# Linear attention and a gated feed-forward in one kernel: v of the first batch loaded ahead of q, and other piece widths in feed-forward blocks 0 to 3

## Chip, cores and metric

The kernel runs on one core of one Trainium2 chip. The metric is the device time of one execution in microseconds (us). The engines of a core work side by side, each through its own instructions in order: PE multiplies matrices, DVE and ACT do element-wise work, POOL does small work and issues DMAs (loads and stores), SP issues DMAs. PEld is the loading of a matmul's stationary operand.

## The reference

Two parts follow each other. The first is a linear attention over 8 batches of 8 heads, 576 tokens and 64 values per head:

```python
r = np.maximum(x, 0.0)                                   # phi, for q and k
return np.concatenate([r * c, r * s], axis=-1)           # c, s: cos and sin of the position
kv = np.einsum('bhsf,bhsd->bhfd', k_p, v)
z = np.sum(k_p, axis=2)
num = np.einsum('bhsf,bhfd->bhsd', q_p, kv)
den = np.einsum('bhsf,bhf->bhs', q_p, z)[..., None] + 1e-06
return (num / den).astype(np.float32)
```

The second is a gated feed-forward over all 8 x 576 = 4608 tokens, 512 wide inside and 1536 in the middle:

```python
rms = np.sqrt(np.mean(x * x, axis=-1, keepdims=True) + 1e-06)
xn = x / rms * rms_g
g = xn @ w_gate
silu = g * (1.0 / (1.0 + np.exp(-g)))
val = xn @ w_val
return (silu * val @ w_out).astype(np.float32)
```

## The kernel before

**Token tiles and blocks.** A batch is cut into four token tiles of 128 tokens, (b, 0) to (b, 3), and a fifth of 64 tokens; the fifths of two batches make one tile. The four full tiles of a batch are one block of 512 tokens for the feed-forward, so blocks 0 to 7 are batches 0 to 7, and block 8 holds the fifths.

**Attention of a batch.** k, q and v come in by two DMAs each (line 117), one for the odd and one for the even partitions. The k features (`k_feat`, lines 246 and 248) and casts of v (`v_cast`, 258 and 260) go to bf16; `kv_mm` (293) multiplies them over the five tiles, `kv_evict` (307, 309, 312) copies the product from PSUM (the memory that PE writes) to SBUF. `q_feat` makes the q features of one tile and one of two halves (cos or sin) on ACT or DVE; `q_turn_pe` (329) transposes them with PE and `q_evict` (338, 340) copies the result; later tiles use a DMA transpose instead (318). `num_mm` (353) makes numerator and denominator of a tile.

**From there to the feed-forward.** `divide` (379, 382, 391: three instructions on DVE), `sumsq` (402 on ACT, then a power on POOL, 407, whose result is called rs), `norm` (412 on DVE, giving xn), then a transpose of xn: `x_turn_pe` with PE (430) and its copy `x_evict` (437 on DVE, 439 on ACT), or `x_turn` as a DMA transpose issued by SP (420). The result, xnT, is what the feed-forward multiplies.

**Feed-forward.** A block has twelve steps, numbered through: step g is step g mod 12 of block g // 12. A step makes one PSUM bank of 512 columns for the gate (gps) and one for the value (vps). In blocks 0 to 4 a step is split by the table `PARTS` (464): an entry (n, first token, tokens) says that the step takes the tokens given and as many rows of 128 features from n on as fill the bank, so four for 128 tokens, two for 256. A matmul is then 128 or 256 columns wide. In blocks 5 to 8 a step is one row of features over all 512 tokens (449). After the matmuls ACT takes silu of gps (696), DVE multiplies by vps (706) into hT. From block 2 on, each step also does four matmuls of the block before it with wo (`out_mm`, 496), whose results ACT copies (502) and SP stores (486). Between blocks 0 and 1 stands `lead` (719), in which the output of block 0 is worked out while batch 1's attention is made ready.

**Order.** Every instruction stays where the program puts it on its engine. For the steps there is a plan: `at(g, kind, f, ...)` puts f into step g at a place named by its kind. The places in a step are, in order: sp, act0, dve0, the gate matmuls, mid, the first half of the value matmuls, half, the second half, silu, act1, act2, dve1, the multiply into hT, pe. Whatever f issues goes to its own engines at that point of their order, so a step's dve0 comes after the multiply of the step before, and its act1 after its own silu. `tile_at(g, ...)` puts num at the end of step g, divide and sumsq into g + 1, norm and the DMA transpose into g + 2.

**Memory that sets waits.** The gate and value banks come from a ring of three banks, which the PE transposes of block 0 use too (`gv_tile`); a bank is free for the next user when its reader is done. One further bank, acc, holds the warm-up matmuls and later the output sums. Each weight comes in by DMAs that POOL issues (`load_gv`, `load_wo`), after a small copy (`pool_after`, 240) that makes POOL wait for a given feature.

Of the kernel before, what the change touches and what calls it, by code (L numbers as in the profile page):

```python
# [17 lines left out]
def kernel(  # L18
# [105 lines left out]
    def load_v(b, cuts=(0, NC5)):  # L124
        load(vraw[b], v, b, False, cuts)

    def load_k(b):
        load(kraw[b], k, b)

    def load_q(b, cuts=(0, NC5)):  # L130
        load(qraw[b], q, b, b % 2 == 1, cuts)
# [3 lines left out]
    clear_fifth(vbuf[0], nc.vector)  # L135
    gb = consts.tile([P, DM], FP32, name="gb")
    load_k(0)
    load_q(0, (0, 2))
    load_v(0)
    K(nc.sync.dma_start(  # L140
        out=gb[:, :], in_=moe_rms_g.rearrange("(o d) -> o d", o=1).to_broadcast([P, DM])
    ))
# [77 lines left out]
    wo = consts.tile([P, NNT, DM], BF16, name="wo")  # L220
    probe = consts.tile([1, 1], BF16, name="probe")
    NG = 3
    GC = DFF // NG
    n4 = NNT // NG

    def load_gv(c):
        for (w, src) in ((wg, moe_w_gate), (wv, moe_w_val)):
            K(nc.gpsimd.dma_start(
                out=w[:, :, c * GC : (c + 1) * GC],
                in_=src[:, c * GC : (c + 1) * GC].rearrange("(t p) n -> p t n", p=P),  # L230
            ))

    def load_wo(c):
        K(nc.gpsimd.dma_start(
            out=wo[:, c * n4 : (c + 1) * n4, :],
            in_=moe_w_out[c * n4 * P : (c + 1) * n4 * P, :].rearrange("(t p) m -> p t m", p=P),
        ))

    def pool_after(src):
        K(nc.gpsimd.tensor_copy(out=probe[:, :], in_=src))  # L240
# [60 lines left out]
    def kv_evict(b):  # L301
        dst = kvm[b % NK][:, :, :].rearrange("p (z s) w -> p z s w", z=2)
        if b == 0:
            for z, t in enumerate(kvp.pop(b)):
                src = t[:, 0 : Z * E].rearrange("p (s w) -> p s w", w=E)[:, :, 0 : D + 1]
                if z == 0:
                    K(nc.scalar.copy(out=dst[:, z, :, 0 : D + 1], in_=src))
                else:
                    K(nc.vector.tensor_copy(out=dst[:, z, :, 0 : D + 1], in_=src))
                gv_read(t)  # L310
        else:
            K(nc.scalar.copy(
                out=dst[:, :, :, 0 : D + 1], in_=att_heads(kvp.pop(b))[:, :, :, 0 : D + 1]
            ))
# [7 lines left out]

    qtp = {}

    def q_turn_pe(b, t):
        ps = gv_tile([P, H, P], BF16, "qtp")
        qp = qps.pop((b, t))
        for h in range(H):
            K(nc.tensor.transpose(  # L329
                ps[:, h, :], qp[:, h, :, :].rearrange("p c d -> p (c d)"), ident_b[:, :]  # L330
            ))
        qtp[b, t] = ps
# [90 lines left out]

    xps = {}

    def x_turn_pe(key):
        ps = gv_tile([P, NDT, P], BF16, "xps")
        xn = xns.pop(key)
        for dt in range(NDT):
            K(nc.tensor.transpose(ps[:, dt, :], xn[:, dt * P : (dt + 1) * P], ident_b[:, :]))  # L430
        xps[key] = ps
# [21 lines left out]
        return ps  # L453

    HB = TB // 2

    def gv_mm_part(w, name, blk, n0, c0, cn, half=None):

        ps = gv_tile([P, TB], FP32, name)
        for i in range(TB // cn):  # L460
            if half is not None and 2 * i == TB // cn:
                half()
            for dt in range(NDT):
                K(nc.tensor.matmul(  # L464
                    ps[:, i * cn : (i + 1) * cn],
                    lhsT=w[:, dt, (n0 + i) * P : (n0 + i + 1) * P],
                    rhs=xnT[blk][:, dt, c0 : c0 + cn],
                    start=(dt == 0), stop=(dt == NDT - 1),
                ))
        return ps  # L470
# [40 lines left out]
    def at(g, w, f, *a):  # L511
        plan[g, w].append(lambda: f(*a))
# [32 lines left out]
        at(g + 1, "act0", kv_evict, b)  # L545


    at(0, "half", x_turn_pe, (0, 1))
    at(0, "act0", sumsq, (0, 2))
    at(0, "dve0", q_feat, 0, 3, 1)  # L550
    at(0, "act1", x_evict, (0, 1), 0, 1)
    at(0, "pe", norm, (0, 2))
    at(0, "pe", q_turn_pe, 0, 3)
    at(1, "act0", q_evict, 0, 3)
    at(1, "mid", x_turn_pe, (0, 2))
    at(1, "dve1", x_evict, (0, 2), 0, 2, True)
    at(1, "mid", num_mm, (0, 3))
    at(1, "dve1", divide, (0, 3))
    at(2, "act0", sumsq, (0, 3))
    at(3, "dve0", norm, (0, 3))  # L560
    at(3, "pe", x_turn_pe, (0, 3))
    at(4, "dve0", x_evict, (0, 3), 0, 3, True)
    for c in range(2):
        at(2 + c, "act2", q_feat, 0, J, c, True)
# [42 lines left out]
    pe_tile_at(19, (2, 0), 2, 0, 22, "act0")  # L607
    for t, g in enumerate((14, 16, 20, 21, 23)):
        q2_at(g, 2, t)
    pe_tile_at(22, (2, 1), 2, 1, 24)  # L610
    tile_at(24, (2, 2), 2, 2)
    tile_at(26, (2, 3), 2, 3)

# [44 lines left out]
    def run(g, w):  # L658
        for f in plan[g, w]:
            f()  # L660


    T = [(c * P, P) for c in range(J)] + [(hf * HB, HB) for hf in range(2)]
    PARTS = {0: tuple((n,) + T[c] for n, c in (
        (0, 0), (0, 1), (0, 2), (4, 4), (6, 4), (0, 3), (4, 5), (6, 5), (8, 4), (10, 4), (8, 5),
        (10, 5),
    ))}
    for blk in (1, 2, 3, 4):
        head = (
            [(n,) + T[c] for c in range(2) for n in (0, 4, 8)] if blk < 3  # L670
            else [(n,) + T[4] for n in range(0, NNT, 2)]
        )
        PARTS[blk] = tuple(head + [(n,) + T[5] for n in range(0, NNT, 2)])

    def step(blk, nn):
        g = blk * NNT + nn
        run(g, "sp")
        run(g, "act0")
        run(g, "dve0")
        while late_turns:  # L680
            x_turn(*late_turns.pop(0))
        if nn == 0:
            hT[blk] = htp.tile([P, NNT, TB], BF16, name="hT", tag="hT")
        if blk in PARTS:
            n0, c0, cn = PARTS[blk][nn]
            ni = TB // cn
            gp = gv_mm_part(wg, "gps", blk, n0, c0, cn)
            run(g, "mid")
            vp = gv_mm_part(wv, "vps", blk, n0, c0, cn, lambda: run(g, "half"))
            dst = hT[blk][:, n0 : n0 + ni, c0 : c0 + cn]  # L690
        else:
            gp = gv_mm(wg, "gps", blk, nn)
            vp = gv_mm(wv, "vps", blk, nn)
            dst = hT[blk][:, nn, :]
        sil = ring(silp, 3, [P, TB], BF16, "sil")
        K(nc.scalar.activation(out=sil[:, :], in_=gp[:, :], func=AF.Silu))  # L696
        gv_read(gp)
        run(g, "act1")
        ends = blk > 1 and nn % 3 == 2
        if not ends:  # L700
            run(g, "act2")
# [70 lines left out]
    def warm_up(n):  # L772
        for _ in range(n):
            K(nc.tensor.matmul(
                wps[:, 0 : 2 * P], lhsT=warm[:, 0:P], rhs=warm[:, :], start=True, stop=True
            ))

    warm_up(44)
    for j in range(NC5):
        for c in range(2):  # L780
            if (j, c) in ((2, 1), (NC5 - 1, 1)):
                q_feat(0, 0, int(j > 2), act=(j > 2))
            k_feat(0, j, c, act=(j > 2))
    for c in range(2):
        q_feat(0, 1, c, act=(c == 1))
    pool_after(qps[0, 0][0:1, 0, 0, 0:1])
    for c in range(NG):
        load_gv(c)
    for c in range(2):
        load_wo(c)  # L790
    q_turn_pe(0, 0)
    q_evict(0, 0, dve=True)
    q_turn_pe(0, 1)
    q_evict(0, 1)
    warm_up(6)
    for j in range(NC5):
        v_cast(0, j, act=(j % 2 == 1))
    for j in (0, 1, 2, 4, 3):
        kv_mm(0, j, j == 0, j == 3)
    kv_evict(0)  # L800
    num_mm((0, 0))
    num_mm((0, 1))
    for c in range(2):
        q_feat(0, 2, c, act=True)
    divide((0, 0))
    warm_up(5)
    q_turn_pe(0, 2)
    warm_up(5)
    sumsq((0, 0))
    divide((0, 1))  # L810
    sumsq((0, 1))
    q_evict(0, 2, dve=True)
    norm((0, 0))
    num_mm((0, 2))
    q_feat(0, 3, 0, act=True)
    x_turn_pe((0, 0))
    divide_rec((0, 2))
    x_evict((0, 0), 0, 0, dve=True)
    divide((0, 2))
    norm((0, 1))  # L820


# [53 lines left out]
```

## Time and profile before

| | |
|---|---|
| time, median of 3 runs | 331.35 us (331.07 to 331.37) |
| the profiled execution's own time | 331.03 us |
| its span, first to last instruction | 328.9 us |
| PE busy in the span | 97% |
| first weight matmul (line 464) | 19.82 us |
| lead begins | 42.67 us |
| granted TensorE clock, mean | 0.999 |

A line of the timeline reads: start, duration, engine, source line, operation, what it writes and reads, shapes, and how many instructions were merged (x8). A bracket at the end tells how long the engine had been idle before, and what released it. In the chain of waits a line is start, duration, and what the chain went through. In a table by stretches the columns are the stretch, its length, busy time and number of instructions of PE, PEld, DVE, ACT and POOL, the granted clock, the share of DMA time and the GB/s. In the list of DMA issues the last figure is the median time in us from issue to landing.

### The profile page before, as it was taken

To read this page: it belongs to the slowest core of one execution; us is meant where nothing else is said; L and a number is where in the kernel's file an instruction comes from. 1 tells how busy PE (TensorE), PEld (TensorE's weight loads), DVE (VectorE), ACT (ScalarE), POOL (GpSimd) and SP (SyncE) were. 2 spreads that over 40 slices of the span, in tenths; PEclk is the share of its full clock that TensorE was granted. 3 is DMA by queue.
4 is the path that set the end of the run, shared out by engine and by line. 5 is a ranking of instruction groups with operands and counts; after the bars stand their busy time and mean duration, and the time that the engine had idled before them with its cause. 6 is when DMAs were issued, how large, how long until landed. Compare 5 with 4: busy or idle time off the path is not lost.

```text
span 328.9 us, 7190 instructions
## 1 busy us (share of the span) xinstructions
PE 318.6 (97%) x2840; PEld 210.5 (64%) x2840; DVE 189.7 (58%) x394; ACT 168.2 (51%) x319; POOL 40.3 (12%) x80
## 2 busy tenths in 40 slices
PE   6789999999999999999999999999999999999995
PEld 4679855999888777778777644454444444444443
DVE  4785386868875676678867685746542422223200
ACT  2865377776576466666645663644332323322221
POOL 3743351100100100001110001100100000000000
PEclk9999999999999999999999999999999999999999
DMA  7999999389469999997799895255124010000012
GB/s 215 305 206 207 287 335 385 121 200 229 148 127 261 319 256 324 189 302 177 205 185 288 174 228 142 65 91 118 49 65 111 33 49 32 35 32 32 34 64 96
DMA packets 83313, 55.26 MB, mean 168 GB/s; under 512 B 51760, under 2 KB 77120, under 8 KB 83280
## 3 DMA queue, kind: packets, MB, share of 16 engines
q1 hardware_dynamic: 76576, 42.88, 52.7%
q0 software_dynamic: 6544, 11.80, 14.8%
q8 instruction: 22, 0.36, 0.4%
q14 instruction: 11, 0.09, 0.1%
q10 hardware_dynamic: 160, 0.13, 0.1%
HBM read 38.01 MB, written 9.44 MB: 144 GB/s over the span
## 4 chain that ended last, share of the span: by engine, by line
PE 89%; DVE 4%; ACT 2%; issue 2%; DMA 2%; SPq 0%; POOL 0%; ACTq 0%; DVEq 0%
PE acc L496 26%; PE gps L464 15%; PE vps L464 15%; PE vps L449 13%; PE gps L449 13%; PE att L353 3%; PE att L293 3%; DMA kbuf<-in_k_dram 2%; DVE xn L412 1%; PE acc L838 1%; PE qtp L329 1%; PE xps L430 1%; ACT kp L246 1%; DVE x L391 1%; DVE kp L248 0%
## 5 line engine op out<-in xcount | busy, mean ns | idle before, releaser
L706 DVE TENSOR_TENSOR hT<-vps,sil 128x512 bf16<-128x512 f32 x108 | 74.5, 690 | 96.3 <-PE vps L449 62.0
L696 ACT ACTIVATE sil<-gps 128x512 bf16<-128x512 f32 x108 | 64.4, 596 | 98.5 <-PE gps L449 60.1
L496 PE MATMUL acc<-wo,hT 128*128 128x512 bf16 x420 | 105.7, 380 | 0.2 <-ACT osb L502 0.2
L496 PEld LDWEIGHTS <-hT 128*128 128x128 bf16 x420 | 40.5, 98 | 40.3 <-issue 0.3
L464 PE MATMUL gps<-xnT,wg 128*128 128x256 bf16 (+1 forms) x608 | 62.5, 250 | 0.5 <-DVE xnT L437 0.5
L464 PE MATMUL vps<-xnT,wv 128*128 128x256 bf16 (+1 forms) x608 | 62.7, 250 | 0.0
L464 PEld LDWEIGHTS <-wg 128*128 128x128 bf16 x608 | 48.0, 98 | 7.7 <-issue 0.6
L464 PEld LDWEIGHTS <-wv 128*128 128x128 bf16 x608 | 49.4, 98 | 4.0
L407 POOL TENSOR_TENSOR rs<-ss,mhalf 128x1 f32<-128x1 f32 x36 | 20.2, 562 | 199.9 <-ACT sq L402 199.9
L449 PE MATMUL vps<-xnT,wv 128*128 128x512 bf16 x144 | 37.0, 379 | 0.0
L449 PE MATMUL gps<-xnT,wg 128*128 128x512 bf16 x144 | 36.9, 379 | 0.0
L502 ACT COPY osb<-acc 128x512 f32<-128x512 f32 x35 | 20.4, 584 | 31.8 <-PE acc L496 30.5
L449 PEld LDWEIGHTS <-wv 128*128 128x128 bf16 x192 | 18.8, 98 | 22.7
L412 DVE SCALAR_TENSOR_TENSOR xn<-x,rs,gb 128x512 bf16<-128x512 f32 x36 | 27.0, 749 | 9.0 <-POOL rs L407 8.8
L449 PEld LDWEIGHTS <-wg 128*128 128x128 bf16 x192 | 18.0, 98 | 20.1
L402 ACT ACTIVATE sq<-x 128x513 f32<-128x513 f32 x36 | 22.6, 629 | 8.6 <-DVE x L391 8.4
L391 DVE TENSOR_TENSOR x<-att,rec 128x512 f32<-128x512 f32 x36 | 24.9, 691 | 1.2
L248 DVE TENSOR_SCALAR kp<-kbuf,trig 128x512 bf16<-128x512 f32 x50 | 22.6, 483 | 3.6 <-DMA kbuf<-in_k_dram 3.2
L248 DVE TENSOR_SCALAR qp<-qbuf,trig 128x512 bf16<-128x512 f32 x50 | 22.9, 481 | 0.0
L246 ACT ACTIVATE kp<-kbuf,trig 128x512 bf16<-128x512 f32 x30 | 20.8, 715 | 3.0 <-DMA kbuf<-in_k_dram 3.0
L246 ACT ACTIVATE qp<-qbuf,trig 128x512 bf16<-128x512 f32 x30 | 21.1, 712 | 0.2 <-DMA qbuf<-in_q_dram 0.2
L353 PEld LDWEIGHTS <-rqT 128*128 128x128 bf16 x320 | 14.4, 98 | 8.0 <-DVE rqT L338 0.9
(64 smaller groups left out, 182.6 us busy)
## 6 DMA issues: line engine op xcount, KB each, us to landing
out_dram<-osb SPq DMA_DIRECT2D x70, 128.0 KB, 2.1
kbuf<-in_k_dram SPq DMA_DIRECT2D x6, 640.0 KB, 5.7
vbuf<-in_v_dram SPq DMA_DIRECT2D x5, 640.0 KB, 7.7
kbuf<-in_k_dram SPq DMA_DIRECT2D x6, 512.0 KB, 4.7
qbuf<-in_q_dram SPq DMA_DIRECT2D x6, 512.0 KB, 5.0
vbuf<-in_v_dram SPq DMA_DIRECT2D x5, 512.0 KB, 6.6
qbuf<-in_q_dram SPq DMA_DIRECT2D x4, 640.0 KB, 6.5
wg<-in_moe_w_gate_dram POOLq DMA_DIRECT2D x3, 512.0 KB, 11.4
```

What stands on the lines that cost most here:

```text
L246: K(nc.scalar.activation(out=dst, in_=src, func=AF.Relu, scale=scale))
L248: K(nc.vector.tensor_scalar(out=dst, in0=src, scalar1=scale, scalar2=0.0, op0=ALU.mult, op1=ALU.max,))
L353: K(nc.tensor.matmul(nums[key][:, h // Z, (h % Z) * E : (h % Z) * E + D + 1], lhsT=rqT[a, t][:, h, :], rhs=kvm[a % NK][:, h, 0 : D + 1], s ...
L391: K(nc.vector.tensor_tensor(out=x[:, 0:DM].rearrange("p (z s d) -> p z s d", z=2, d=D), in0=a[:, :, :, 0:D], in1=r.unsqueeze(3).to_broadca ...
L402: K(nc.scalar.activation(out=sq[:, :], in_=xs[key][:, :], func=AF.Square, scale=1.0 / math.sqrt(DM), accum_out=ss[:, :],))
L412: K(nc.vector.scalar_tensor_tensor(out=xn[:, :], in0=xs.pop(key)[:, 0:DM], scalar=rss.pop(key)[:, :], in1=gb[:, :], op0=ALU.mult, op1=ALU. ...
L449: K(nc.tensor.matmul(ps[:, :], lhsT=w[:, dt, nn * P : (nn + 1) * P], rhs=xnT[blk][:, dt, :], start=(dt == 0), stop=(dt == NDT - 1),))
L464: K(nc.tensor.matmul(ps[:, i * cn : (i + 1) * cn], lhsT=w[:, dt, (n0 + i) * P : (n0 + i + 1) * P], rhs=xnT[blk][:, dt, c0 : c0 + cn], star ...
L496: K(nc.tensor.matmul(acc[blk][:, :], lhsT=hT[blk][:, nn, jt * P : (jt + 1) * P], rhs=wo[:, nn, :], start=(nn == 0), stop=(nn == NNT - 1),))
L502: K(nc.scalar.copy(out=osb[:, :], in_=acc[blk][:, :]))
L696: K(nc.scalar.activation(out=sil[:, :], in_=gp[:, :], func=AF.Silu))
L706: K(nc.vector.tensor_tensor(out=dst, in0=a, in1=c, op=ALU.mult))
```

## The change

On SP the load of v of batch 0 stands ahead of the first columns of q. The first features and casts are in another order: all of k, then v's casts and kv, then the q features of tiles (0,0) and (0,1), then `kv_evict`, whose halves also swap engines. The first weights come in pieces of 256 columns (two rows of features), four for each of the two matrices, and the remaining third and the first two of wo are issued later. The probe that releases them reads a k feature instead of a q feature. Warm-up matmuls are set anew (52, 3, 12 instead of 44, 6, 5, 5).

In block 0 the first step is a pair: rows 0 and 1 over tokens 0 to 127, and then, in the same step and banks, over tokens 128 to 255 (`gv_mm_pair`). Into its first half go num of tile (0,2) and the transpose of tile (0,1). The three PE transposes of xn and the q transpose planned in block 0's steps use the bank acc instead of the ring. Divide of (0,3) moves from step 1's dve1 to step 2's dve0.

The table of pieces: block 1 has a pair, then five steps of 256 tokens from the first half, then six of the second; block 2 has four 128-token steps instead of six; block 3 has three steps of tokens 0 to 255, three of tokens 256 to 511, and then six of all 512. Block 4 is as it was.

```diff
     load_k(0)
+    load_v(0)
     load_q(0, (0, 2))
-    load_v(0)
...
-    def load_gv(c):
+    def load_gv(lo, hi):
+
+        cs = slice(lo * P, hi * P)
...
+    def gv_mm_pair(blk, n0, between, half):
+
+        gp, vp = (gv_tile([P, TB], FP32, name) for name in ("gps", "vps"))
+        for c in range(2):
+            for w, ps in ((wg, gp), (wv, vp)):
+                if c == 0 and w is wv:
+                    between()
+                for i in range(2):
+                    if c == 0 and w is wv and i == 1:
+                        half()
+                    for dt in range(NDT):
+                        K(nc.tensor.matmul(
+                            ps[:, i * HB + c * P : i * HB + (c + 1) * P],
+                            lhsT=w[:, dt, (n0 + i) * P : (n0 + i + 1) * P],
+                            rhs=xnT[blk][:, dt, c * P : (c + 1) * P],
+                            start=(dt == 0), stop=(dt == NDT - 1),
+                        ))
+        return gp, vp
...
-    at(0, "half", x_turn_pe, (0, 1))
-    at(0, "act0", sumsq, (0, 2))
-    at(0, "dve0", q_feat, 0, 3, 1)
-    at(0, "act1", x_evict, (0, 1), 0, 1)
-    at(0, "pe", norm, (0, 2))
-    at(0, "pe", q_turn_pe, 0, 3)
-    at(1, "act0", q_evict, 0, 3)
-    at(1, "mid", x_turn_pe, (0, 2))
-    at(1, "dve1", x_evict, (0, 2), 0, 2, True)
-    at(1, "mid", num_mm, (0, 3))
-    at(1, "dve1", divide, (0, 3))
-    at(2, "act0", sumsq, (0, 3))
+    at(0, "mid", num_mm, (0, 2))
+    at(0, "half", x_turn_pe, (0, 1), True)
+    at(0, "half", x_evict, (0, 1), 0, 1)
+    at(0, "half", divide, (0, 2))
+    at(0, "half", sumsq, (0, 2))
+    at(0, "half", q_feat, 0, 3, 1)
+    at(0, "act2", q_turn_pe, 0, 3, True)
+    at(0, "act2", q_evict, 0, 3)
+    at(0, "dve1", norm, (0, 2))
+    at(1, "half", x_turn_pe, (0, 2), True)
+    at(1, "half", x_evict, (0, 2), 0, 2)
+    at(1, "pe", num_mm, (0, 3))
+    at(2, "dve0", divide, (0, 3))
+    at(2, "act1", sumsq, (0, 3))
     at(3, "dve0", norm, (0, 3))
-    at(3, "pe", x_turn_pe, (0, 3))
+    at(3, "pe", x_turn_pe, (0, 3), True)
...
-    pe_tile_at(22, (2, 1), 2, 1, 24)
+    pe_tile_at(22, (2, 1), 2, 1, 24, "act0")
...
+    PARTS = {
+        0: parts((0, PAIR), (2, 4), (0, 2), (4, 4), (6, 4), (0, 3), (4, 5), (6, 5), (8, 4),
+                 (10, 4), (8, 5), (10, 5)),
+        1: parts((0, PAIR), *over(4, 2, NNT), *over(5, 0, NNT)),
+        2: parts(*over(0, 0, 8), *over(1, 0, 8), *over(4, 8, NNT), *over(5, 0, NNT)),
+        3: parts(*over(4, 0, 6), *over(5, 0, 6), *over(6, 6, NNT)),
+        4: parts(*over(4, 0, NNT), *over(5, 0, NNT)),
+    }
...
-    warm_up(44)
+    warm_up(52)
     for j in range(NC5):
         for c in range(2):
-            if (j, c) in ((2, 1), (NC5 - 1, 1)):
-                q_feat(0, 0, int(j > 2), act=(j > 2))
             k_feat(0, j, c, act=(j > 2))
-    for c in range(2):
-        q_feat(0, 1, c, act=(c == 1))
-    pool_after(qps[0, 0][0:1, 0, 0, 0:1])
-    for c in range(NG):
-        load_gv(c)
-    for c in range(2):
-        load_wo(c)
+    pool_after(kp[2][0:1, 0, 1, 0:1])
+    for lo in range(0, 2 * n4, 2):
+        load_gv(lo, lo + 2)
+    for j in range(NC5):
+        v_cast(0, j, act=(j % 2 == 1))
+    for j in (0, 1, 2, 4, 3):
+        kv_mm(0, j, j == 0, j == 3)
+    for t in range(2):
+        for c in range(2):
+            q_feat(0, t, c, act=(c == 1))
+    kv_evict(0)
...
+    warm_up(12)
+    q_turn_pe(0, 2)
+    q_evict(0, 2)
+    load_gv(2 * n4, NNT)
+    for c in range(2):
+        load_wo(c)
     norm((0, 0))
...
```

In the table, the second number of an entry stands for its tokens: 0 to 3 one tile, 4 the first and 5 the second 256 tokens, 6 all 512, and 7 (`PAIR`) the pair.

More of the change, by code (lines that the diff above doesn't have):

```diff
@@ L222 @@
     NG = 3
-    GC = DFF // NG
     n4 = NNT // NG
-    def load_gv(c):
+    def load_gv(lo, hi):
+        cs = slice(lo * P, hi * P)
         for (w, src) in ((wg, moe_w_gate), (wv, moe_w_val)):
             K(nc.gpsimd.dma_start(
-                out=w[:, :, c * GC : (c + 1) * GC],
-                in_=src[:, c * GC : (c + 1) * GC].rearrange("(t p) n -> p t n", p=P),
+                out=w[:, :, cs], in_=src[:, cs].rearrange("(t p) n -> p t n", p=P)
             ))
@@ L305, in kv_evict @@
                 src = t[:, 0 : Z * E].rearrange("p (s w) -> p s w", w=E)[:, :, 0 : D + 1]
-                if z == 0:
+                if z == 1:
                     K(nc.scalar.copy(out=dst[:, z, :, 0 : D + 1], in_=src))
@@ L323, with turn_tile, q_turn_pe @@
     qtp = {}
-    def q_turn_pe(b, t):
-        ps = gv_tile([P, H, P], BF16, "qtp")
+    def turn_tile(shape, name, spare):
+        if spare:
+            return ps_acc.tile(shape, BF16, name=name, tag="acc")
+        return gv_tile(shape, BF16, name)
+    def q_turn_pe(b, t, spare=False):
+        ps = turn_tile([P, H, P], "qtp", spare)
         qp = qps.pop((b, t))
@@ L424, with x_turn_pe @@
     xps = {}
-    def x_turn_pe(key):
-        ps = gv_tile([P, NDT, P], BF16, "xps")
+    def x_turn_pe(key, spare=False):
+        ps = turn_tile([P, NDT, P], "xps", spare)
         xn = xns.pop(key)
@@ L660, in run, with parts, over @@
             f()
[L663 to L673, printed above, removed]
+    T = [(c * P, P) for c in range(J)] + [(hf * HB, HB) for hf in range(2)] + [(0, TB), (0, 0)]
+    PAIR = 7
+    def parts(*a):
+        return tuple((n,) + T[c] for n, c in a)
+    def over(c, lo, hi):
+        w = TB // T[c][1]
+        return [(n, c) for n in range(lo, hi, w)]
+    PARTS = {
[6 more added lines that the diff above has]
+    }
     def step(blk, nn):
@@ L685, in step @@
             n0, c0, cn = PARTS[blk][nn]
+            mid, half = (lambda w=w: run(g, w) for w in ("mid", "half"))
+            if cn == 0:
+                gp, vp = gv_mm_pair(blk, n0, mid, half)
+                cn = HB
+            else:
+                gp = gv_mm_part(wg, "gps", blk, n0, c0, cn)
+                mid()
+                vp = gv_mm_part(wv, "vps", blk, n0, c0, cn, half)
             ni = TB // cn
-            gp = gv_mm_part(wg, "gps", blk, n0, c0, cn)
-            run(g, "mid")
-            vp = gv_mm_part(wv, "vps", blk, n0, c0, cn, lambda: run(g, "half"))
             dst = hT[blk][:, n0 : n0 + ni, c0 : c0 + cn]
@@ L794 @@
     q_evict(0, 1)
[L795 to L800, printed above, removed]
     num_mm((0, 0))
+    warm_up(3)
     num_mm((0, 1))
-    for c in range(2):
-        q_feat(0, 2, c, act=True)
+    q_feat(0, 2, 0, act=True)
     divide((0, 0))
-    warm_up(5)
-    q_turn_pe(0, 2)
-    warm_up(5)
     sumsq((0, 0))
@@ L811 @@
     sumsq((0, 1))
-    q_evict(0, 2, dve=True)
+    q_feat(0, 2, 1)
+    warm_up(12)
[4 more added lines that the diff above has]
+        load_wo(c)
     norm((0, 0))
-    num_mm((0, 2))
-    q_feat(0, 3, 0, act=True)
     x_turn_pe((0, 0))
-    divide_rec((0, 2))
+    q_feat(0, 3, 0)
     x_evict((0, 0), 0, 0, dve=True)
-    divide((0, 2))
     norm((0, 1))
```

## The prediction

> **What bounds the kernel now.** I read the page first, then the chain of waits and the timeline of the first 45 us, then the timelines of PE and SP in blocks 1 to 5, and last the landing times of the transposes. The page's busy times and its chain by engine:
>
> ```profile
> PE 318.6 (97%) x2840; PEld 210.5 (64%) x2840; DVE 189.7 (58%) x394; ACT 168.2 (51%) x319; POOL 40.3 (12%) x80
> ...
> PE 89%; DVE 4%; ACT 2%; issue 2%; DMA 2%; SPq 0%; POOL 0%; ACTq 0%; DVEq 0%
> ```
>
> PE is the bound from the first weight matmul to the end. Only three things can move the time: when that matmul starts, how long PE needs for the same products, and new waits of PE. The chain ahead of the start:
>
> ```profile
> 12.73 0.63 ACT vx L258
> ...
> 14.92 0.49 PE att L353 x8
> ...
> 17.51 0.68 DVE rqT L338
> 18.19 0.67 DVE xn L412
> 18.86 0.05 issue
> 18.91 0.41 PE xps L430 x4
> 19.32 0.02 issue
> 19.34 0.44 DVE xnT L437
> ```
>
> So v's landing (its first cast is at 12.39) leads through kv, num, divide, norm and transpose to the first weight matmul at 19.82. Block 0, lead and block 3 on the timeline (start, duration, engine, line):
>
> ```profile
> 28.43 0.39 PE L430 MATMUL xps<-ident_b,xn 128*128 128x128 bf16 x4
> ...
> 42.67 4.05 PE L496 MATMUL acc<-wo,hT 128*128 128x512 bf16 x18
> ...
> 119.73 1.95 SPq L420 DMA_TRANSPOSE xnT<-xn  x1
> ...
> 124.05 1.04 PE L464 MATMUL gps<-xnT,wg 128*128 128x256 bf16 x8
> ...
> 133.15 1.04 PE L464 MATMUL gps<-xnT,wg 128*128 128x256 bf16 x8
> ```
>
> 28.43 is the transpose of tile (0,3), which PE makes at the end of step 3 without a wait; 42.67 is the lead. 119.73 is the DMA transpose of tile (3,3), the last quarter of block 3's tokens; 124.05 is step 39, 133.15 step 42. The landing of that transpose, asked for alone:
>
> ```profile
> xnT<-xn SPq DMA_TRANSPOSE x1, 7.3
> ```
>
> 119.73 + 7.3 = 127.0. Before, tokens 256 to 511 of block 3 are read from step 42 on, 6 us later.
>
> **Widths.** One pass over one weight takes, from start to start, 0.894 us in 128-column matmuls (62.00, 62.90, 63.79), 0.8725 in 256 (75.05, 75.92, 76.79) and 0.865 in 512 (186.00, 186.87). A step has two passes: 128 to 256 saves 0.044, 256 to 512 saves 0.015. Block 1 gets 5 wider steps (0.22), block 2 gets 2 (0.09), block 3 gets 6 of 512 (0.09): -0.4 us, all on PE. The step saved in block 0 is in the next part. In blocks 1 and 2 the tiles are there in time: (2,1), now read from step 26 (87.42), is copied before the silu at 85.92; the pair of block 1 reads tiles copied by 57.9, its step starts at 58.18.
>
> **Block 3.** Its steps are now three of tokens 0 to 255, three of tokens 256 to 511, then the wide ones. Step 39 therefore reads tile (3,3). Its norm, its place on SP behind v's load of batch 5 (118.26) and that load stay where they are against PE's steps. It lands at 127.0 and step 39 wants it at 124.05: PE waits 3.0 us. Nothing gives this back: after 58 us the page's groups leave PE 0.2 us of waits (161.75). Bounds: the other transposes of blocks 1 to 4 landed 2.4 to 8.2 us after issue, which is no wait up to 3.9. The row is that of the very transpose, with the same load ahead, so I take 3.0. Tile (3,2), landed at 122.9, is in time.
>
> **The start of block 0.** SP: v moves ahead of two q loads, and those behind two v loads. The queue moves the same bytes by the time that k, v and q's first columns are in, so q's columns land when v did, 12.34, or a little sooner; v lands at about 10.25 (1.18 MB behind k, at about 370 GB/s, and the 0.95 by which k's landing trailed its bytes). gb and the rest of q keep their places: 15.0. For q's first columns I take 12.2, bounds 11.9 and 12.5.
>
> From there by rows of the first 23 us. The eight more warm-up matmuls end at 10.4, ahead of kv; the probe that releases POOL's weight DMAs reads a k feature ready at 9.8, as its q feature was. v's casts and kv are done at 12.35; but kv_evict now stands behind four q features on both engines. ACT: features 12.25 to 13.58, copy of kv to 13.87. PE: turns to 13.62 and 14.24 (0.61 each); copies on DVE (0.69) to 14.34, on ACT (1.01) 14.26 to 15.27. num 14.39, divide (1.13) to 15.96, sumsq and its read (0.73) to 16.78, POOL (0.57) to 17.43, norm (0.74) to 18.25, transpose (0.40), copy (0.42) to 19.16: first weight matmul at 19.22, 0.6 earlier than before. POOL's eight weight issues (0.78 each from 10.19) end at 16.5, 0.4 ahead of its first rs; at 0.92 each, the dearest in the rows, they would end at 17.6 and cost 0.6.
>
> Then the pair. Half a pass, num (0,2), a quarter pass, transpose (0,1) at 20.14; its copy on ACT ends at 21.15, where PE stands at 20.59: a wait of 0.6. Second half to 22.1, turn (0,3) to 22.55, step 1 with transpose (0,2) at 23.86. Behind it, in order: ACT copies it (24.29 to 24.87), only then silu of step 1 (25.39), multiply (26.11), and only then divide (0,3), which was ahead of the multiply: 27.16; sumsq behind silu 2, 27.98; POOL 28.63; norm 29.45. PE has finished step 3 at 28.46 and stands before transpose (0,3) until 29.51: 1.05 of wait, against 28.43 before. All that follows in block 0, and the lead, is 1.1 us later. The same sums on the old order give 28.34 for 28.43. With q's bounds this is +0.8 to +1.4, with POOL's dearest issue +1.7.
>
> **Weight pieces, by rule and row.** The 256-column pieces are eight DMAs instead of four for the same bytes. POOL waits at its ninth DMA or later for an old landing (its q load at 28.54 waited for a wg piece, the one eight places back); now rs of tile (0,2), wanted at 22.14, stands behind DMAs that wait for the first four pieces. Those are the bytes of the first two pieces before, landed at 20.7: the twelfth is out at 21.5. Packets of 1362 bytes took 59.7 ns, of 642 bytes 32.1 (16 engines, 10 to 12 and 12 to 14 us): halved ones of 1 KB read would take 38.9 to 46.7 ns where two of 2 KB took 77.8 each, so up to 20% more: 22.5, and rs 0.3 late. Transpose (0,2) has 0.3 to spare. I take 0. The first two pieces, half the bytes of those that landed at 17.4 and 20.7, are in before 19; the last four weight and first two wo DMAs, now behind two rs, still follow in the same order, and batch 1's k, out by about 25.5 instead of 24.5, has until the lead. The Trainium skill ("DMA: Bandwidth & Descriptors", Specifications) puts the smallest transfer at line rate at 512 bytes, which these writes just reach; by that the cost is 0 too, and by the rows' line at most 0.1.
>
> **Sum.** +1.1 - 0.4 + 3.0 = +3.7 on the profiled execution's 331.03 (span 328.9 and 2.1 around it) is 334.7. That execution is 0.3 under the median of 331.35: 335.1.
>
> **Rivals.**
>
> (a) No wait in block 3, the one that ends on the other side: the transpose lands within 4.3 us of its issue, as those at 89.05, 95.75 and 112.14 did (2.4, 2.5, 3.9). Against: they had no load of 1.15 MB just ahead on SP. It gives 332.05; with q's columns at 11.9, 331.75, which is not slower.
>
> (b) The lead takes up most of the late start: PE stands there for some 0.85 us in all (0.28 ahead of 46.84, 0.19 of 51.14, 0.12 of 55.47, 0.26 of 57.04, with 0.216 for each matmul of 512 columns before). That holds if landings, not PE's order, set the lead. For: v of batch 1 lands just before 47.44. Against: ACT starts the lead's k features at 42.49, straight after its last silu. It gives 334.2.
>
> (c) PE's clock drops after the wait of 3 us. Row: PE ran 7 warm matmuls from 4 to 5 us and 12 from 8 to 9, after a start at 2.81, so the slow stretch is some 4 us and costs 2. No wait in this trace is above 0.9 us once it is warm, so none shows a drop or excludes one. It gives 337.1.
>
> ```profile
> 4.00:5.00 1.00, 1.00 (x7) 0.67 (x6) 0.10 (x1) 0.22 (x1) 0.00 (x0) 1.00 1.08 388
> 8.00:9.00 1.00, 1.00 (x12) 0.89 (x10) 1.00 (x4) 1.00 (x3) 0.00 (x0) 1.00 1.11 324
> ```
>
> The Trainium skill ("TensorE: Matmul & The Clock Gate", Part 1) has the clock halved after a whole idle window of about 3.4 us; a 3.0 us wait stays just under it, and a longer one would not.
>
> (d) Earlier start without both waits: -0.6 - 0.4, 330.3. It would need ACT and DVE to be a microsecond shorter at two places.
>
> **Chances.** Forecast 0.70, (a) 0.11, (b) 0.08, (c) 0.07, (d) 0.04. What a measurement of this kernel can tell from no change is about 0.2%, 0.66 us. Slower: 0.70 + 0.08 + 0.07 and half of (a), 0.91; within: half of (a), 0.05; faster: (d), 0.04. The forecast's own bounds: landing of (3,3) half a microsecond either way, start +0.8 to +1.7: 334.3 to 336.2. With (b) and the upper half of (a) it holds 8 in 10: 332.0 to 336.4.
>
> **What would show it.** First weight matmul near 19.2; a PE wait of 0.6 for ACT's xnT copy near 21 and of about 1 for DVE's xn near 29; lead near 43.8; passes of 0.87 in block 1; in block 3 a PE wait of about 3 us before its fourth step. It is wrong if that wait is absent, or if tile (0,3) does not stop PE.

## The result, and the profile after

The changed kernel takes 333.75 us, the median of six executions (333.64 to 334.31), against 331.08 us for the kernel before (330.92 to 331.37): a ratio of 1.0082, with an interval of 1.0069 to 1.0095. It is slower by 2.67 us. The prediction was 335.1 us, with a range of 332.0 to 336.4.

The profiled execution of the changed kernel is the slowest of its six: 334.31 us, with a span of 332.5 us (the other five spans are 331.9 to 332.1). Its span is 3.6 us longer than the 328.9 of before. The shares by engine on the chain that ended last, from the page after:

```profile
PE 83%; DMA 6%; DVE 5%; issue 2%; ACT 2%; POOL 1%; SPq 0%; ACTq 0%; DVEq 0%
```

PE had 89% of that chain before and DMA 2%. Waits for DMAs have therefore come into the chain, and the chain in order of time says which. First its head, up to the first weight matmul (start, duration, what it went through):

```profile
4.38 8.23 DMA qbuf<-in_q_dram
...
12.70 0.73 ACT qp L246
...
14.13 0.70 DVE rqT L344
...
18.79 0.41 PE xps L436 x4
...
19.23 0.44 DVE xnT L443
...
19.70 0.61 PE gps L474 x8
```

The chain now begins with q's first columns (in at 12.6), no longer with v. v's casts begin at 10.9 instead of 12.39. The first weight matmul is at 19.70, 0.12 earlier than before. Next, PE's timeline after, with its waits in brackets:

```profile
21.68 0.61 PE L474 MATMUL gps<-xnT,wg 128*128 128x128 bf16 x8 [0.45 <-ACT xnT L445]
...
29.91 0.40 PE L436 MATMUL xps<-ident_b,xn 128*128 128x128 bf16 x4 [0.82 <-DVE xn L418]
...
44.16 4.05 PE L521 MATMUL acc<-wo,hT 128*128 128x512 bf16 x17
...
119.01 1.05 PE L489 MATMUL gps<-xnT,wg 128*128 128x256 bf16 x8 [1.43 <-DMA xnT<-xn]
...
127.80 1.05 PE L489 MATMUL gps<-xnT,wg 128*128 128x256 bf16 x8 [0.78 <-DMA xnT<-xn]
```

Four of these lines have a wait, two in block 0 and two in block 3. 29.91 answers to 28.43 of before and 44.16 (the lead) to 42.67: they are 1.48 and 1.49 us later, so all of block 0's loss is there by the transpose of tile (0,3). 119.01 is step 36, which begins block 3, and 127.80 is step 39. The landings in question, in us after the issue, for tile (3,1), issued at 113.65, and for tile (3,3), issued at 121.42:

```profile
xnT<-xn SPq DMA_TRANSPOSE x1, 5.3
xnT<-xn SPq DMA_TRANSPOSE x1, 6.3
```

They land at 118.95 and 127.7, each just ahead of the step that waits. Step by step, the start times in the two traces differ like this:

| place | before | after | difference | added since the row above |
|---|---|---|---|---|
| step 4 (after the transpose of (0,3)) | 28.66 | 30.14 | +1.48 | +1.48 |
| step 12 (block 1) | 58.18 | 59.66 | +1.48 | 0 |
| step 24 (block 2) | 81.64 | 82.92 | +1.28 | -0.20 |
| step 30 | 99.54 | 100.74 | +1.20 | -0.08 |
| step 36 (block 3) | 116.22 | 119.01 | +2.79 | +1.59 |
| step 39 | 124.05 | 127.80 | +3.75 | +0.96 |
| step 48 (block 4) | 151.33 | 154.97 | +3.64 | -0.11 |

Outside the span the execution after has 1.8 us (334.31 - 332.5), the one before 2.1. That is why 3.6 us of span are only 3.3 us between the two profiled executions.

### The profile page after: what moved, and what is told of

The parts are those of the page before. It is cut to its first block, busy times and chain, and to the rows that moved or that the text cites. A ratio compares the mean times of both kernels' runs of the same rounds, so it can differ in the third digit from the quotient of the medians.

```text
span 332.5 us, 6823 instructions
## 1 busy us (share of the span) xinstructions
PE 316.9 (95%) x2637; PEld 204.3 (61%) x2671; DVE 190.3 (57%) x394; ACT 168.8 (51%) x319; POOL 43.0 (13%) x84
## 4 chain that ended last, share of the span: by engine, by line
PE 83%; DMA 6%; DVE 5%; issue 2%; ACT 2%; POOL 1%; SPq 0%; ACTq 0%; DVEq 0%
PE acc L521 24%; PE gps L489 13%; PE vps L489 12%; PE gps L455 12%; PE vps L455 12%; DMA xnT<-xn 4%; PE att L293 3%; PE att L359 3%; DMA qbuf<-in_q_dram 2%; DVE xn L418 1%; PE qtp L335 1%; PE acc L874 1%; PE xps L436 1%; ACT sq L408 1%; DVE x L397 1%
## 5 line engine op out<-in xcount | busy, mean ns | idle before, releaser
L521 PE MATMUL acc<-wo,hT 128*128 128x512 bf16 x399 | 102.4, 379 | 1.3 <-ACT osb L527 0.2
L489 PE MATMUL gps<-xnT,wg 128*128 128x256 bf16 (+2 forms) x486 | 60.1, 267 | 2.4 <-DMA xnT<-xn 2.2
L489 PE MATMUL vps<-xnT,wv 128*128 128x256 bf16 (+2 forms) x488 | 60.4, 267 | 0.0
L489 PEld LDWEIGHTS <-wg 128*128 128x128 bf16 x488 | 42.3, 98 | 11.5 <-DMA xnT<-xn 3.2
L489 PEld LDWEIGHTS <-wv 128*128 128x128 bf16 x488 | 43.9, 98 | 7.0
L455 PEld LDWEIGHTS <-wv 128*128 128x128 bf16 x192 | 18.8, 98 | 22.6
L455 PEld LDWEIGHTS <-wg 128*128 128x128 bf16 x192 | 18.0, 98 | 20.1
L248 DVE TENSOR_SCALAR qp<-qbuf,trig 128x512 bf16<-128x512 f32 x52 | 24.1, 486 | 0.5 <-DMA qbuf<-in_q_dram 0.5
L246 ACT ACTIVATE qp<-qbuf,trig 128x512 bf16<-128x512 f32 x28 | 19.7, 713 | 0.7 <-DMA qbuf<-in_q_dram 0.7
```

Source lines behind the costliest of these rows:

```text
L246: K(nc.scalar.activation(out=dst, in_=src, func=AF.Relu, scale=scale))
L248: K(nc.vector.tensor_scalar(out=dst, in0=src, scalar1=scale, scalar2=0.0, op0=ALU.mult, op1=ALU.max,))
L455: K(nc.tensor.matmul(ps[:, :], lhsT=w[:, dt, nn * P : (nn + 1) * P], rhs=xnT[blk][:, dt, :], start=(dt == 0), stop=(dt == NDT - 1),))
L489: K(nc.tensor.matmul(ps[:, i * cn : (i + 1) * cn], lhsT=w[:, dt, (n0 + i) * P : (n0 + i + 1) * P], rhs=xnT[blk][:, dt, c0 : c0 + cn], star ...
L521: K(nc.tensor.matmul(acc[blk][:, :], lhsT=hT[blk][:, nn, jt * P : (jt + 1) * P], rhs=wo[:, nn, :], start=(nn == 0), stop=(nn == NNT - 1),))
```

## The experiments

Two questions came from this table. What makes step 36 wait, which the prediction did not see? And are block 0, the tables and block 3 really separate terms? Times below are medians, and each ratio is taken to the kernel before in the runs of the same round on the same chip. Its median was 331.02 in the round of block 3's two tables, of the tables of blocks 1 and 2, and of the divide alone; 331.15 in the round of block 1's table, of the two kernels with tiles (3,1) and (3,3) on PE, and of the load order; and 331.32 in the round of the other four.

**Which part makes which wait in block 3.** The changed kernel with block 3's old table:

```diff
-        3: parts(*over(4, 0, 6), *over(5, 0, 6), *over(6, 6, NNT)),
+        3: parts(*over(4, 0, NNT), *over(5, 0, NNT)),
```

> The changed kernel with block 3's pieces as they were (all of tokens 0 to 255 first, in 256 columns). In the changed kernel PE waits 1.6 us for a transpose at step 36 and 0.95 at step 39. Theory A: the new table of block 3 makes both waits; they go, the 0.09 of the 512-column pieces is lost, and the time is 333.75 - 2.55 + 0.09 = 331.3. Theory B: only the wait at step 39 is the table's, since step 36 reads tokens 0 to 255 in both tables; the first wait stays and the time is 333.75 - 0.95 + 0.09 = 332.9, with 1.6 us of wait at step 36.

332.72 us, ratio 1.0056 (1.0043 to 1.0069). PE's timeline of this kernel has one wait left in block 3, at step 36:

```profile
118.00 1.05 PE L489 MATMUL gps<-xnT,wg 128*128 128x256 bf16 x8 [0.96 <-DMA xnT<-xn]
```

The new table costs the wait at step 39, as predicted, but not the one at step 36. The reverse edit puts block 3's new table, and nothing else, into the kernel before:

```diff
+        3: parts(*over(4, 0, 6), *over(5, 0, 6), *over(6, 6, NNT)),
```

> The kernel before with block 3's new pieces alone. Theory A (tokens 256 to 511 are now read at step 39, before tile (3,3) has landed): PE waits 2.5 to 3.0 us in all in block 3, 0.09 is saved by width: 333.5 to 334.0. Theory B (the head's delay, not the table, makes the transposes late): at most 1 us of wait, 331.1 to 332.0.

333.78 us, ratio 1.0098 (1.0065 to 1.013); two of the six executions had a mean clock of 0.992 and took 335.83 and 336.58 us, the profiled one had 0.999 and took 333.43. PE's timeline of this kernel:

```profile
126.57 1.05 PE L489 MATMUL gps<-xnT,wg 128*128 128x256 bf16 x8 [2.16 <-DMA xnT<-xn]
```

Alone, the table makes the wait as the prediction described it, at step 39 and nowhere else. Tile (3,3) lands 6.6 us after its issue at 119.93. In the changed kernel the wait at step 39 is shorter because step 36 has already held PE up; by the brackets the two waits there make 1.43 + 0.78 = 2.21, hardly more than this one.

The kernel before with the new tables of blocks 1 and 2, and with tile (2,1)'s copy ahead of the silu as these need it (block 3's table as before):

```diff
+        1: parts((0, PAIR), *over(4, 2, NNT), *over(5, 0, NNT)),
+        2: parts(*over(0, 0, 8), *over(1, 0, 8), *over(4, 8, NNT), *over(5, 0, NNT)),
```

> The kernel before with the new pieces of blocks 1 and 2 alone (and tile (2,1)'s copy moved with them). Theory A: only the width counts, 7 steps by 0.044: -0.3, 330.8, and step 36 starts without a wait. Theory B: quicker steps of block 2 let PE reach step 36 before tile (3,1) has landed, which landed 0.2 us ahead of it before: a wait there of up to 1.6 us, 331 to 332.4.

332.03 us, ratio 1.003 (1.0007 to 1.0053). Step 35 starts at 113.22 instead of 113.61, and 0.12 of that is there at step 12 already (58.06 against 58.18), so the widths did give 0.27 us. Then PE's timeline of this kernel has, at step 36:

```profile
117.06 1.05 PE L489 MATMUL gps<-xnT,wg 128*128 128x256 bf16 x8 [1.08 <-DMA xnT<-xn]
```

The gain of the wider pieces was more than taken back by the wait for tile (3,1): +1.01 us against before in the medians, 1.3 away from the -0.27. The kernel before has these lines for that tile, its landing and step 36:

```profile
112.14 1.22 SPq L420 DMA_TRANSPOSE xnT<-xn  x1
...
xnT<-xn SPq DMA_TRANSPOSE x1, 3.9
...
116.22 1.04 PE L464 MATMUL gps<-xnT,wg 128*128 128x256 bf16 x8
```

The tile landed at 112.14 + 3.9 = 116.04, only 0.18 us ahead of step 36. In the kernel with the new tables it is issued at 111.78, 0.36 earlier, and lands at 117.0, almost a microsecond later. With block 1's table alone:

```diff
+        1: parts((0, PAIR), *over(4, 2, NNT), *over(5, 0, NNT)),
```

> The kernel before with block 1's new pieces alone. Theory A: the late landing of tile (3,1)'s transpose (5.2 us after issue with the new pieces of blocks 1 and 2, 3.9 without) comes from block 2's pieces, right ahead of it: here it lands after 3.9, no wait at step 36, 331.02 - 0.22 = 330.8. Theory B: any shift of PE's steps against the DMA queue does it: wait of about 1.1 at step 36, 331.9.

332.64 us, ratio 1.0037 (1.0024 to 1.005). PE's timeline of this kernel has that wait again, and a smaller one at step 48:

```profile
117.37 1.05 PE L489 MATMUL gps<-xnT,wg 128*128 128x256 bf16 x8 [1.30 <-DMA xnT<-xn]
152.92 1.05 PE L489 MATMUL gps<-xnT,wg 128*128 128x256 bf16 x8 [0.27 <-DMA xnT<-xn]
```

Tile (3,1) was issued at 111.83 and landed 5.5 us later. So the landing of this tile is not a constant of the kernel: 3.9 us in the kernel before and with block 3's table alone, 5.2 or more here. Block 1's new table by itself is enough to bring the late landing, although that block ends before 82 us.

What happens while the tile is on its way stands in the DMA traffic (queue, packets, MB, share of 16 engines, which passes 100% when packets overlap). In the changed kernel, between 116.5 and 117.0 and then between 117.0 and 117.5:

```profile
q1 hardware_dynamic: 507, 0.13, 428.2%
q8 instruction: 1, 0.02, 12.6%
...
DMA packets 2, 0.00 MB, mean 4 GB/s; under 512 B 0, under 2 KB 2, under 8 KB 2
```

In the kernel before, between 115.0 and 115.5, there is no such instruction DMA and the traffic flows:

```profile
DMA packets 533, 0.15 MB, mean 303 GB/s; under 512 B 503, under 2 KB 533, under 8 KB 533
```

The queue that the profile names instruction moves 16 KB, and behind it nearly all other DMA traffic of the core stops for about a microsecond; packets caught by it took up to 1.4 us each in the changed kernel. Eleven traces make this transpose by DMA. In the nine with the late landing (5.2 to 5.5 us), a q8 DMA starts 1.3 to 3.2 us after the issue; in the two with 3.9 us it starts 7.3 and 7.5 us after it, when the tile has landed. How block 1's table can reach so far is then an inference: the page of before counts 22 of these DMAs for 2840 matmuls of PE, about one in 130; with that table PE has 2760, and the tenth such DMA comes at 113.14 instead of 102.95. No run moved this DMA and nothing else, so the link is read from the traces and not tested.

**Taking the DMA transposes away.** In the changed kernel, PE transposes tiles (3,1) and (3,3), four more 128-column transposes each:

```diff
-        tile_at(g, (3, t), 3, t)
+        if t % 2:
+            pe_tile_at(g, (3, t), 3, t, g + 2)
+        else:
+            tile_at(g, (3, t), 3, t)
```

> The changed kernel with the token tiles (3,1) and (3,3) transposed by PE and copied by ACT instead of by a DMA transpose; block 3's pieces are the new ones. Theory A: the waits at steps 36 and 39 (2.2 to 2.5 us) are for the landing of these two DMA transposes; both go, two PE transposes cost 0.23 each: 333.75 - 2.4 + 0.46 = 331.8, and no PE wait in block 3. Theory B: the tiles are late before their transpose (norm or SP behind them): PE then waits in the transposes themselves, and the time stays above 333.

332.03 us, ratio 1.0019 (1.0003 to 1.0035), and PE's timeline has no wait between 105 and 155 us. The two waits are worth 1.8 us (2.67 - 0.88), after paying for the eight transposes.

The same mend at tile (3,1) alone, in the kernel before with the tables of blocks 1 and 2:

```diff
+        if t == 1:
+            pe_tile_at(g, (3, t), 3, t, g + 2)
+        else:
+            tile_at(g, (3, t), 3, t)
```

> The kernel before with the new tables of blocks 1 and 2, as in the earlier run before_tab12 (332.03), and tile (3,1) transposed by PE instead of by DMA (4 transposes, 0.23 of PE more than the matmuls around it need). Theory A (the widths pay, and what took their gain was the wait for tile (3,1) alone): 331.15 - 0.31 + 0.3 = 331.1, no wait in block 3. Theory B (something else of the tables costs): 332.0 again.

331.15 us, ratio 0.9993 (0.9981 to 1.0005), against 1.003 without the mend. So that wait was what the tables cost. What is left of the gain by widths, less the price of four transposes, is too small for the medians to tell from nothing.

**Do the loads on SP set the landings?** In the changed kernel, batch 5's k, v and q are loaded later, so that v no longer stands ahead of tile (3,3), and k not right behind (3,1):

```diff
-            5: ((33, 35, 36), (41, 42, 43, 44, 45), 46, 45, (49, 51, 53, 55)),
+            5: ((37, 37, 38), (41, 42, 43, 44, 45), 46, 45, (49, 51, 53, 55)),
```

> Only edit: batch 5's loads of k, v and q are issued at steps 37, 37 and 38 instead of 33, 35 and 36, so none of them stands on SP ahead of the transpose of tile (3,3), and k's no longer right behind that of tile (3,1). Theory A (a load ahead of a DMA transpose on SP delays its landing): (3,3) lands 2.4 to 4 us after its issue instead of 6.3, the wait of 0.95 at step 39 goes: 332.8; if k's load behind (3,1) is what stretches its landing from 3.9 to 5.3, the wait at step 36 (1.6) goes too: about 331.3. Theory B (the landing does not depend on these loads, but on when PE's steps come): both waits stay, 333.75.

338.86 us, ratio 1.0224 (1.021 to 1.0238): much slower, which neither theory said. Within block 3 the trace still answers the question. The landing of tile (3,3), issued at 118.98 in this kernel:

```profile
xnT<-xn SPq DMA_TRANSPOSE x1, 2.4
```

With v's load ahead it was 5.6 to 7.3 us in ten traces; without it 2.4, and the wait at step 39 is gone. The edit also takes q's load away from right behind this tile, so it does not separate the two by itself; but tile (3,2), which had k's load just ahead and no load right behind, lands after 4.2 us here against 7.0 in the changed kernel. Tile (3,1) still lands 5.3 us after its issue and step 36 still waits (1.22), so k's load behind it is not the cause there. The loss is in block 4. SP's timeline in this kernel:

```profile
132.91 9.92 SPq L318 DMA_TRANSPOSE rqT<-qp  x4
...
147.04 1.51 SPq L426 DMA_TRANSPOSE xnT<-xn  x1
...
149.93 3.79 SPq L318 DMA_TRANSPOSE rqT<-qp  x1
153.81 1.22 SPq L426 DMA_TRANSPOSE xnT<-xn  x1
```

The transpose of q at 149.93 holds SP for 3.79 us; SP's waits put 3.6 of that down to PE's num (line 359). The transpose of tile (4,1) stands behind it and is issued at 153.81, against 149.40 in the changed kernel. PE waits at step 48, and then its matmuls are slow:

```profile
158.02 1.13 PE L489 MATMUL gps<-xnT,wg 128*128 128x256 bf16 x8 [4.50 <-DMA xnT<-xn]
158.94 1.91 PE L489 MATMUL vps<-xnT,wv 128*128 128x256 bf16 x8
160.65 1.83 PE L521 MATMUL acc<-wo,hT 128*128 128x512 bf16 x4
```

The table by stretches for this kernel shows the granted clock (third figure from the right):

```profile
158.00:159.00 1.00, 0.98 (x9) 0.86 (x10) 0.00 (x0) 0.00 (x0) 0.00 (x0) 0.92 1.15 330
159.00:160.00 1.00, 1.00 (x6) 0.70 (x5) 0.00 (x0) 0.82 (x2) 0.00 (x0) 0.50 0.84 164
160.00:161.00 1.00, 1.00 (x6) 0.61 (x4) 0.04 (x1) 1.00 (x4) 0.53 (x1) 0.50 0.96 184
161.00:162.00 1.00, 1.00 (x4) 0.38 (x3) 0.65 (x1) 0.51 (x1) 0.02 (x1) 0.50 0.24 47
162.00:163.00 1.00, 1.00 (x14) 0.73 (x13) 0.20 (x2) 0.00 (x0) 0.00 (x0) 0.87 0.81 159
```

The same loads with all three new tables on the kernel before (its own block 0) were the attempt at a kernel faster than both:

```diff
-            5: ((33, 35, 36), (41, 42, 43, 44, 45), 46, 45, (49, 51, 53, 55)),
+            5: ((37, 37, 38), (41, 42, 43, 44, 45), 46, 45, (49, 51, 53, 55)),
+        1: parts((0, PAIR), *over(4, 2, NNT), *over(5, 0, NNT)),
+        2: parts(*over(0, 0, 8), *over(1, 0, 8), *over(4, 8, NNT), *over(5, 0, NNT)),
+        3: parts(*over(4, 0, 6), *over(5, 0, 6), *over(6, 6, NNT)),
```

> The kernel before with all three new tables (blocks 1, 2, 3) and batch 5's loads of k, v and q at steps 37, 37 and 38; block 0, its load order and its first weight pieces as before. Widths are worth -0.40. Theory A (the loads of batch 5 make the transposes late): no wait in block 3, 331.15 - 0.40 = 330.75, faster than both kernels. Theory B (the landings stay late whatever the loads): about 1.1 at step 36 and about 1.3 at step 39, 333.2.

337.65 us, ratio 1.019 (1.0175 to 1.0205). The same picture: 1.22 at step 36, none at step 39 (the tile lands 2.5 us after its issue), 3.97 at step 48, and matmuls at half the clock after it.

**Block 0.** In the changed kernel, num of (0,3) goes back into the middle of step 1, and divide ahead of that step's multiply:

```diff
-    at(1, "pe", num_mm, (0, 3))
-    at(2, "dve0", divide, (0, 3))
-    at(2, "act1", sumsq, (0, 3))
+    at(1, "half", num_mm, (0, 3))
+    at(1, "dve1", divide, (0, 3))
+    at(2, "act0", sumsq, (0, 3))
```

> The changed kernel with num of tile (0,3) in step 1's half, its divide ahead of step 1's multiply and its sumsq ahead of step 2's silu, as the order was before the change. Theory A: the wait ahead of the transpose of tile (0,3) (0.8 us in the changed kernel) is made by divide standing behind that multiply; it goes, 333.75 - 0.85 = 332.9, lead at 43.3. Theory B: another wait takes its place (silu of step 2 now behind sumsq holds a bank), and less than 0.3 is won: 333.4 to 333.8.

332.87 us, ratio 1.0054 (1.0042 to 1.0066), 0.8 less than the changed kernel. PE no longer waits before the transpose of (0,3), and step 4 is at 28.80. The waits in block 3 stay (1.40 and 0.78 by the brackets), although step 35 now starts at 113.58, level with the 113.61 of before: the wait at step 36 is no mere matter of how far PE's steps have shifted. With this and the two PE transposes of block 3 together:

```diff
-    at(1, "pe", num_mm, (0, 3))
-    at(2, "dve0", divide, (0, 3))
-    at(2, "act1", sumsq, (0, 3))
+    at(1, "half", num_mm, (0, 3))
+    at(1, "dve1", divide, (0, 3))
+    at(2, "act0", sumsq, (0, 3))
-        tile_at(g, (3, t), 3, t)
+        if t % 2:
+            pe_tile_at(g, (3, t), 3, t, g + 2)
+        else:
+            tile_at(g, (3, t), 3, t)
```

> The changed kernel with both mends: divide of (0,3) ahead of step 1's multiply, and tiles (3,1) and (3,3) transposed by PE. Theory A: the two gains are independent, 332.87 - 2.2 + 0.46 = 331.1, level with the kernel before. Theory B: the DMA queue rid of two transposes speeds other landings too, or slack hidden so far shows up: 330.6 or less.

331.02 us, ratio 0.9989 (0.9975 to 1.0003). The two mends add up: 0.82 and 1.79 by themselves, 2.80 together, where the change had lost 2.67. The change with both is level with the kernel before, not shown to be faster.

The load order alone undone, q's first columns ahead of v again:

```diff
-    load_v(0)
     load_q(0, (0, 2))
+    load_v(0)
```

> The changed kernel with q's first columns loaded ahead of v, as before the change; the order of the engines' work stays the new one. Theory A: the new order needs v early, since casts and kv stand ahead of the q features; v lands at 12.3 instead of 10.8, the q features end after the casts at about 14.9 instead of 14.0, and the first weight matmul moves from 19.4 to 20.3: +0.9, 334.6. Theory B: the start hangs on q's last columns or on POOL, not on v: no change, 333.6 to 333.9.

335.67 us, ratio 1.0118 (1.0094 to 1.0143): 1.9 worse than the changed kernel, where 0.9 was expected. The direction holds: the new order of features needs v first. The rest goes with a lower clock. PE's timeline of this kernel has the wait for v's casts, and the table by stretches what comes after:

```profile
12.83 1.68 PE L293 MATMUL kv<-vx,kp 128*128 128x65 bf16 x40 [1.95 <-DVE vx L260]
```

```profile
13.00:14.00 1.00, 1.00 (x32) 0.94 (x30) 1.00 (x3) 1.00 (x2) 1.00 (x3) 1.00 1.11 315
14.00:15.00 1.00, 1.00 (x21) 1.00 (x18) 0.96 (x3) 0.97 (x3) 1.00 (x3) 0.61 1.42 211
15.00:16.00 1.00, 1.00 (x12) 0.97 (x10) 0.58 (x1) 0.00 (x0) 1.00 (x2) 0.50 1.45 195
```

The one of its four executions that kept a mean clock of 1.0 took 334.63 us, which is the expected 0.9 more than 333.75. The three at 0.992 to 0.995 took 335.4 to 336.1.

The first weights in 512-column pieces again:

```diff
-    for lo in range(0, 2 * n4, 2):
-        load_gv(lo, lo + 2)
+    for lo in range(0, 2 * n4, n4):
+        load_gv(lo, lo + n4)
```

> The kernel after with the first weights loaded in pieces of 512 columns again, four DMAs instead of eight. Theory A (the narrow pieces cost and gain nothing): within 0.3 of 333.75, first weight matmul at 19.7, no PE wait for wg or wv beyond 0.3. Theory B (the narrow pieces cost POOL or bandwidth time in block 0): the lead comes up to 0.6 earlier and the time is 333.1.

333.76 us, ratio 1.0067 (1.0051 to 1.0082). No difference from the changed kernel, so the narrow pieces cost nothing that shows. In this trace q's features start at 12.24, the first weight matmul at 19.23, and PE then waits 0.45 for wv at 20.55, more than was expected; with the narrow pieces no trace has that wait.

## Why the prediction was right, point by point

**The side, and the mechanisms.** Slower was right, and the three named waits are all there: PE for ACT's copy of (0,1), PE for the norm of (0,3), PE for the transpose of (3,3). Undoing the divide's move, or block 3's table, took each of the last two away by itself.

**Widths, -0.4.** The table of step starts adds up to -0.20, -0.08 and -0.11, together -0.39, against the predicted -0.22, -0.09 and -0.09.

**The start, +1.1.** In the profiled execution it was +1.48, because q's first features start at 12.70 and not at 12.2. That fits a spread of that landing between executions, of which the profiled one is the slowest: in the changed kernel with block 3's old table, q's features start at 12.25, the first weight matmul is at 19.24 and the lead at 43.70, where the prediction had 19.22 and 43.8. v landed later than its 10.25 (the casts start at 10.89), which costs nothing as long as q's columns come later still. Behind q's landing the sums held: a bracket of 0.45 for the pair where 0.6 was predicted, one of 0.82 before the transpose of (0,3) where 1.05 was. POOL came as predicted too: its first rs (17.38) and that of tile (0,2) (22.66) waited for ACT's sums, not for DMA issues.

**Block 3, +3.0.** This is the term that was mis-sized, and partly misplaced. It measured 2.55, in two waits: 1.59 at step 36 and 0.96 at step 39. That the sum comes near 3.0 although the first wait was not foreseen is luck: the first wait takes from the second, and the table alone makes one of 2.16 by the bracket. The prediction took the landing of tile (3,3) from its own row (7.3) and was 0.7 to 1.0 us too high (6.3 in the changed kernel, 6.6 with the table alone). For the tiles read at step 36 it said only that nothing after 58 us waits: it did not set the landing of (3,1), 116.04, beside the step that reads it, 116.22. That margin of 0.18 us was visible. Every traced kernel with the new table of block 1 and this DMA transpose used it up, because the tile then landed later after its issue, each time with an instruction DMA in its way. The reading of (3,3) as held back by v's load ahead of it on SP is borne out as far as the runs go: without the loads around it, it landed after 2.4 and 2.5 us.

**Rivals.** (a), no wait in block 3, was wrong. (b), the lead takes up the late start, was wrong: +1.48 goes in and +1.48 comes out. (c), a drop of the clock after the wait, was wrong for this kernel, whose waits were 1.6 and 1.0 and whose mean clock was 0.998 to 1.0 in all six executions; but the mechanism is real (below). (d), the start without both waits, was wrong.

**From the trace to the time.** The prediction's 335.1 is 1.35 over the median. Half a microsecond of that is the term of block 3. Some 0.3 came from adding the difference between the profiled execution and the median of three runs: over six runs the kernel before has 331.08, where the profiled execution had 331.03, so there was hardly anything to add. Another 0.3 is the time outside the span, which was taken as unchanged and became 1.8 instead of 2.1. All profiled kernels with the new block 0 have 1.7 to 1.8 there and all with the old one 2.1 to 2.2; the cause is open. The rest, about 0.3, is not assigned.

## What to carry to other kernels

Before PE's steps are moved by even a fraction of a microsecond, set the landing of each tile beside the step that reads it: a margin of 0.18 us on a DMA landing is none, and an edit that makes PE quicker by 0.3 us came out 1.0 us slower. Look also for instruction DMAs: as the traces suggest, an edit that changes the number of PE's matmuls can put one in the way of a transfer tens of microseconds later. A DMA transpose landed late here when a large load was issued just ahead of it on the same queue (5.6 to 7.3 us against 2.4). But moving such a load moves all that stands behind it on that queue: look up what the next waiting instruction there will block, as the transpose of tile (4,1) was blocked here.

## What the runs showed of the hardware

**Landings of a DMA transpose vary several times over.** The same transpose of one 128-token tile, (3,3), landed 2.4 and 2.5 us after its issue with no load around it and 5.6 to 7.3 with 1.15 MB just ahead on SP. Tile (3,1) landed after 3.9 us in the kernel before and with block 3's table alone, and after 5.2 to 5.5 where block 1's table is new, with k's load behind it or not, and with step 35 anywhere from 0.4 earlier to 2.6 later than before.

**Behind a DMA of instructions the other DMA traffic stopped for about a microsecond.** In the nine traces with (3,1) late, the 16 KB DMA of queue q8 falls into its flight, and packets caught behind it took up to 1.24 to 1.53 us; the landings are 1.3 to 1.6 us later than the 3.9 of the two traces in which it does not.

**The granted clock halves after idle time of PE, for some 3.4 us.** It fell to 0.50 towards the end of a wait of 4.0 us and 0.8 us behind one of 4.5, and once after a wait of only 1.95 us at the start, behind which PE had just the matmuls of kv (65 columns each) and then the turns. The stretches at half clock ran from 155.89 to 159.31, from 158.85 to 162.26 and from 14.22 to 17.63, each 3.4 us. No drop followed the waits of 1.6 in the changed kernel or 2.2 in the trace with block 3's table alone; of that kernel's six executions two had a mean clock of 0.992 and took 335.8 and 336.6 us, the others 332.9 to 334.1 at 0.998 or more. That would fit a wait near the edge, but no trace of those two exists, and the kernel before, whose trace has no such wait, also had one execution of 17 at 0.99 (334.72 us): what dropped the clock there is open. The Trainium skill ("TensorE: Matmul & The Clock Gate", Part 1) has the clock halved after an idle window of about 3.4 us that runs freely. The length of the slow stretches agrees; the drop after 1.95 us of idle is shorter than that rule allows, and here the measurement decides.
